# Late chunks of alpha, k and q landed token by token, with a ScalarE copy beside and transposes that write in order

## The chip, the cores and the metric

The kernel runs on one core of one Trainium2 chip. The metric is the device time of one execution, in microseconds. Numbers of the profile come from one profiled execution on the same chip.

## The reference

A gated linear attention recurrence, for batch 4, 8 heads, 768 tokens and head size 48, is followed by a two-layer block with a SiLU between:

```python
for t in range(S):
    state = alpha[:, :, t, :, None] * state + einsum('bhd,bhe->bhde', k[:, :, t], v[:, :, t])
    y[:, :, t] = einsum('bhd,bhde->bhe', q[:, :, t], state)
x = y.transpose(0, 2, 1, 3).reshape(B * S, H * D)     # 3072 x 384
h = x @ w_in                                          # w_in 384 x 2048
out = (h * (1 / (1 + exp(-h)))) @ w_out               # w_out 2048 x 384
```

q, k, v and alpha are fp32. The two weights arrive as 64-bit floats and are rounded on the chip.

## The kernel before

The tokens are cut into chunks of 128; with 4 batches there are NT = 24 chunks, numbered so that the four batches of one token range follow each other. The function `quotients` holds the whole fast path. Step n of its main loop runs the stages of chunk n (products, quotient, flip) and the later stages of chunk n-1 (land, scores, values, states). Between the stages, `fill` puts pieces of the two-layer block: `enter` (x times w_in, with sums that spare products), `leave` (times w_out). The first NA = 8 chunks are early ones; the 16 from chunk 8 on are late ones, and the change touches only these. The late stage begins with `settle`, which frees buffers of the first stage and makes three tiles, `quads`, one each for alpha, k and q (`at`, `kt`, `qt` in the profile).

**How a late chunk is loaded.** `load(n, name)` is called for each tensor as soon as the tensor of chunk n-1 has been transposed, since there is one tile for each. Line 486 issues four transfers of 96 KB for each tensor. A group of 32 partitions takes four heads of one parity (u); partition b of the group takes the four tokens 4b to 4b+3, so that each run is 4 x 48 elements, 768 bytes. The same data land twice: once in the partitions 64u to 64u+31 from column 32 on, and once in the next 32 partitions from column 0 on, so that the same columns of the two groups hold, for one token, the elements 0 to 31 and the elements from 32 on.

**How it is transposed.** `turned` (line 708) lets VectorE transpose blocks of 32 x 32: for head pair g and token j of the four, 32 partitions by 32 columns. What comes out is the head dimension over the partitions and the tokens along the row. As partition b held the tokens 4b to 4b+3, the results of one block go to every fourth element of the row.

**What comes of it.** `products` takes alpha (scan on line 734: products of decays from the end of the chunk), then k (kp on lines 749 and 751). `quotient` makes the other scan (line 764) and q's product (line 770). `flip` (line 780) transposes kp and writes it to DRAM (line 782, `flips`); in the next step `land` (line 790) reads it back as `kn`, in four transfers, for `states` (line 874), which adds the chunk to the recurrent state. `scores` multiplies kp and qp, ScalarE copies the results from PSUM (lines 818 and 821) and scales the state (line 836), GpSimd masks them (line 825), and `values` makes the chunk's output, which ScalarE copies into `xt` (line 863).

**What sets the order.** Each engine works through its own queue in order. A scheduler places the instructions of the traced program on the queues; from the late stage on, TensorE's matmuls are held in program order. All loads of chunks, the flips, the reads of kn and the loads of `audit` stand in one queue, SyncE's, and each waits there for what its buffer needs. `audit` reads alpha and the weights once more in pieces, from step 15 on, and checks their range with reductions on VectorE (line 697); its later pieces land in the three `quads` tiles. The outputs go through GpSimd's queue (line 1059).

PSUM banks: three for `enter` (ps_m), two for `leave` (ps_o), three for the attention (ps_a). ScalarE empties them with lines 950 (`enter`), 1054, 1073 and 1078 (`leave`) and 923 (the plain form of `enter`, with SiLU); VectorE with lines 958, 1056, 1088 and 1099. Line 1047 makes differences for `leave`.

Of the kernel before, what the change touches and what calls it, by code (L numbers as in the profile page):

```python
# [8 lines left out]
F32 = mybir.dt.float32  # L9
I32 = mybir.dt.int32  # L10
# [345 lines left out]
def quotients(  # L356
# [19 lines left out]
    nc = tc.nc  # L376
    dve, act, gps = nc.vector, nc.scalar, nc.gpsimd

    late = {}
# [14 lines left out]
    B, H, S, D = q.shape  # L394
    C = 128
    NCH = S // C
    NP = H // 2
    HD = H * D
# [3 lines left out]
    NT = B * NCH  # L402
# [9 lines left out]
    def pool(name, bufs=1, space=None):  # L412
        kw = {} if space is None else {"space": space}
        return ctx.enter_context(tc.tile_pool(name=name, bufs=bufs, **kw))
# [40 lines left out]
    NA = 2 * GB  # L455
# [8 lines left out]
    ctxs = {}  # L464

    def load(n, names="akq"):
        if n == NT:
            return
        c = ctxs.setdefault(n, dict(zip(("ci", "b"), divmod(n, B))))
        b, rows = c["b"], slice(c["ci"] * C, c["ci"] * C + C)  # L470
        for name, src in (("a", alpha), ("k", k), ("q", q)):
            if name not in names:
                continue
            x = src[b, :, rows, :]
            if n < NA:
                c[name] = nat[name][n % NIN]
                nc.sync.dma_start(c[name][:, :, 0:D], x.transpose([1, 0, 2]))
                continue

            c[name] = late["quads"][name]
            for u in range(2):
                for i in range(2):
                    r = 64 * u + 32 * i
                    nc.sync.dma_start(
                        c[name][r : r + 32, 32 * (1 - i) :][:, 0 : 4 * NP * D].rearrange(
                            "p (g c) -> p g c", g=NP),
                        x[u::2].rearrange("h (b j) d -> b h (j d)", j=4))

    NV = 2
    vns = [fix.tile([128, H, 64], F32, name=f"vn{i}") for i in range(NV)]
# [3 lines left out]
    def load_v(n):  # L496
        c = ctxs.setdefault(n, dict(zip(("ci", "b"), divmod(n, B))))
        x = v[c["b"], :, c["ci"] * C : c["ci"] * C + C, :].transpose([1, 0, 2])
        t = c["v"] = vns[n % NV]
        if n < NA:  # L500
            nc.sync.dma_start(t[:, :, 0:D], x)
            return
        nc.sync.dma_start(t[:, 0 : H // 2, 0:D], x[:, 0 : H // 2])
        for e in range(2):
            nc.sync.dma_start(t[CH * e : CH * e + CH, H // 2 :, 0:D], x[CH - CH * e : C - CH * e, H // 2 :])
# [7 lines left out]
    def fetch():  # L513

        if wide and sources:
# [4 lines left out]
            coming.append(bits)  # L520

    load(0)
    load(1)
    for i in range(4):
        fetch()
# [47 lines left out]
    quads = w_in.rearrange("p k (q i c) -> p i k q c", i=4, c=128)  # L573
# [83 lines left out]
    def audit():  # L657


        flat = alpha.rearrange("b h s d -> (b h s d)").rearrange("(p c) -> p c", p=128)  # L660
        assert 2 * HD <= 32 + 4 * NP * D
        todo = [(flat[:, c : c + AW], AW, 0) for c in range(0, flat.shape[1], AW)]
        if wide:
            todo += [(moe_w_in[t * 128 : t * 128 + 128, c : c + 512], 512, 1)
                     for c in range(0, DF, 512) for t in range(NKT)]
            todo += [(moe_w_out[f * 128 : f * 128 + 128, :], HD, 1) for f in range(NFT)]
        alone = sum(2 * x[1] > 32 + 4 * NP * D or x[2] == 0 for x in todo)
        for kind in (0, 1):
            n = sum(x[2] == kind for x in todo)
            if n:  # L670
                seen.append([fix.tile([128, n], F32, name=f"seen{kind}{i}") for i in range(2)])
        at = [0, 0]
        landed = []

        def begin(src, n, kind):
            at = len(landed)
            t = late["look"].tile([128, 512, 2], I32, name="bits").rearrange("p n w -> p (n w)") if (
                at < alone) else late["quads"]["akq"[at % 3]].bitcast(I32)
            if kind == 0:
                landed.append(t[:, 0:n].bitcast(F32))  # L680
                nc.sync.dma_start(landed[-1], src)
            else:
                nc.sync.dma_start(t[:, 0 : 2 * n], src.bitcast(I32))
                landed.append(t[:, 0 : 2 * n].rearrange("p (n w) -> p n w", w=2)[:, :, 1])

        for i, (src, n, kind) in enumerate(todo):

            while len(landed) < min(i + (1 if i + 1 < alone else 3), len(todo)):
                begin(*todo[len(landed)])
            x = landed[i]  # L690
            yield
            i = at[kind]
            at[kind] += 1
            for which, op in ((0, ALU.max), (1, ALU.min)):
                if kind == 1 or which == 0:
                    tc.keep_in_program_order(
                        dve.tensor_reduce(seen[kind][which][:, i : i + 1], x, axis=AX, op=op,  # L697
                                          apply_absolute_value=True))
# [5 lines left out]
        return t[:, 1 : NP * W + 1].rearrange("p (j c) -> p j c", c=W)[:, :, 0:C]  # L704

    def turned(x, to):
        x = x[:, 32:].rearrange("p (g j d) -> p g j d", j=4, d=D)
        dve.transpose(to.rearrange("p g (b j) -> p g j b", j=4), x[:, :, :, 0:32])

    def products(n):  # L710

# [28 lines left out]
        if n >= NA:  # L740
            ps["k"] = late["turn"].tile([128, NP, C], F32, name="turn")
            turned(c["k"], ps["k"])
            load(n + 1, "k")
# [414 lines left out]
    def go_on():  # L1158
# [3 lines left out]
        done += 1  # L1162

    audits = audit()
    done, bridged = 0, 0
    STEPS = NT + 1
# [4 lines left out]
    def settle():  # L1171

        first.close()
        late.update(look=pool("look"), part=pool("part"), turn=pool("turn"),
                    xc=pool("xc").tile([128, len(SUMS_X), TB], F32, name="xc"),
                    wx=pool("wx").tile([128, 8, NQ, 128], F32, name="wx"))
        quads = pool("quads")
        late["p"] = pool("p").tile([128, NP * W + 1], F32, name="p")
        late["quads"] = {name: quads.tile([128, 32 + 4 * NP * D], F32, name=f"{name}t") for name in "akq"}
        for name, t in late["quads"].items():  # L1180
            gps.memset(t, 1.0 if name == "a" else 0.0)
        load(NA)

    def fill(step, slot):

        at = step * SLOTS + slot
        if at < marks[0]:
            if at == SLOTS:
                next(conv[0])
            elif step >= 1:  # L1190
                convert(0, (at - SLOTS) * 3 // (marks[0] - SLOTS) + 1)
            return
        i = next(i for i, m in enumerate(marks[1:]) if at < m)
        a, b = [work_at[n] for n in ([0] + phases)[i : i + 2]]
        due = a + (b - a) * (at - marks[i] + 1) / (marks[i + 1] - marks[i])
        if at % 2 == 0 and step > 3 * GB + 2:
            next(audits, None)
        while work_at[done + 1] <= due and pieces[done][2] <= bridged:
            convert(0, 3 * (done // 2) + 6)
            convert(1, 3 * (done - 6) // 2)  # L1200
            go_on()

    for step in range(STEPS):
        if step == 1:
            load(NIN)
        stages = [[(scores, 1)], [(products, 0)], [(values, 1)], [(states, 1)]]
        if step == 1:

            stages = stages[1::-1] + stages[2:]
        elif step >= NA:  # L1210
            stages = [[(land, 1), (scores, 1)], [(products, 0)], [(quotient, 0)],
                      [(values, 1), (states, 1), (flip, 0)]]
        for slot, group in enumerate(stages):
            for stage, lag in group:
                n = step - lag
                if not 0 <= n < NT:
                    continue
                stage(n)
                if stage is values:
                    bridged = n + 1  # L1220
                if stage is states and n + 1 + NIN < NA:
                    load(n + 1 + NIN)
                if stage is states and n + NV < NT:
                    load_v(n + NV)
            if step * SLOTS + slot == (NA + 1) * SLOTS - 1:
                x = decayed.rearrange("p (o i c) -> p o i c", o=2, c=C)
                for r, o in later:
                    gps.memset(x[r, o, :, 0:CH], 0.0)
            fill(step, slot)
            if step * SLOTS + slot >= NA * SLOTS - 1 and conv_done[1] == NFT and not late:  # L1230
                settle()
# [82 lines left out]
```

## Time and profile before

| | us |
|---|---|
| median of 3 runs | 556.63 (556.30 to 557.37) |
| the profiled execution | 557.26 |
| its span, first to last instruction | 555.5 |
| TensorE matmul busy | 541.4 (97%) |
| VectorE busy | 445.4 (80%) |
| ScalarE busy | 208.5 (38%) |
| GpSimd busy | 76.1 (14%) |
| granted TensorE clock | 0.999 |

In the profile PE is TensorE's matmuls, PEld its weight loads, DVE is VectorE, ACT is ScalarE, POOL is GpSimd and SP is SyncE; a q behind an engine means its queue, where DMAs are issued. L708 is line 708 of the kernel. A group of instructions shows its busy time, the mean of one, and how long the engine stood idle just before it and what ended that. A line of waits gives the time in total, how often, and the longest. Idle time of an engine that isn't the bottleneck costs nothing.

### The profile page before, as it was taken

Reading aid. Unit: us, or ns where it says so; the run is one execution under the profiler, and the core shown is the slowest. Engines: PE = TensorE matmul, PEld = TensorE weight load, DVE = VectorE, ACT = ScalarE, POOL = GpSimd, SP = SyncE. Lnnn points to the kernel's source line nnn. Section 1 sums busy time; section 2 is a strip of 40 time slices with the busy share of each in tenths; the row PEclk is TensorE's granted clock in tenths of the full one; section 3 lists DMA queues with packets and bytes.
Section 4 is the critical chain, followed back from the end, with each engine's and each line's share of the span. In section 5 each row is a group of like instructions: output and inputs, shape, how many; then the busy total and the mean of one; then the engine's idle time right before and its main releaser. Section 6 shows DMA issues by size and latency. Waiting matters only on the chain. (4 is left out here: it accounts for less than half of the span.)

```text
span 555.5 us, 12640 instructions
## 1 busy us (share of the span) xinstructions
PE 541.4 (97%) x5026; PEld 489.7 (88%) x5026; DVE 445.4 (80%) x801; ACT 208.5 (38%) x466; POOL 76.1 (14%) x146
## 2 busy tenths in 40 slices
PE   6999999999999999999999999999999999999996
PEld 4788887998899999899999999988998999999996
DVE  5897788974999899997998986998884796945431
ACT  2556653223333253353353353344263342332100
POOL 3210000222210212021011021021121000001000
PEclk9999999999999999999999999999999999999999
DMA  9998971164454625355545654617642135500000
GB/s 215 246 249 210 232 195 33 47 161 116 117 136 125 159 63 138 86 145 149 139 112 139 193 139 120 191 27 183 170 137 91 54 91 169 172 11 22 10 24 30
DMA packets 99217, 70.09 MB, mean 126 GB/s; under 512 B 56272, under 2 KB 88656, under 8 KB 99152
## 3 DMA queue, kind: packets, MB, share of 16 engines
q1 hardware_dynamic: 97232, 65.30, 45.1%
q0 software_dynamic: 1920, 3.93, 2.0%
q8 instruction: 40, 0.66, 0.5%
q14 instruction: 25, 0.20, 0.1%
HBM read 61.34 MB, written 7.86 MB: 125 GB/s over the span
## 5 line engine op out<-in xcount | busy, mean ns | idle before, releaser
L388 PE MATMUL ps_o<-w_out,g 128*128 128x192 f32 x768 | 134.0, 328 | 0.5 <-DVE o L1056 0.5
L388 PEld LDWEIGHTS ps_o<-w_out,g 128*128 128x128 f32 x768 | 125.6, 190 | 3.5 <-DVE o L1056 1.0
L388 PE MATMUL ps_m<-xt,w_in 128*128 128x256 f32 x480 | 113.6, 383 | 1.5 <-ACT xt L863 1.1
L388 PEld LDWEIGHTS ps_m<-xt,w_in 128*128 128x128 f32 x480 | 89.1, 190 | 14.4 <-ACT xt L863 1.6
L388 PE MATMUL ps_o<-wt,g 128*128 128x192 f32 x576 | 99.7, 326 | 0.0
L388 PEld LDWEIGHTS ps_o<-wt,g 128*128 128x128 f32 x576 | 95.1, 190 | 1.6 <-issue 0.2
L388 PE MATMUL ps_m<-xc,w_in 128*128 128x256 f32 x288 | 70.7, 382 | 0.0
L388 PEld LDWEIGHTS ps_m<-xc,w_in 128*128 128x128 f32 x288 | 53.7, 190 | 7.0 <-DVE g L958 0.3
L1047 DVE TENSOR_TENSOR g<-g 128x512 f32<-128x512 f32 x72 | 50.1, 709 | 8.3 <-PE ps_o L388 8.3
L955 ACT ACTIVATE g<-g 128x1024 f32<-128x1024 f32 x32 | 33.1, 1056 | 61.2 <-DVE g L958 61.1
L1059 POOL DMA_DIRECT2D out_dram<-o x40 | 22.0, 551 | 219.5 <-DVE o L1056 113.7
L825 POOL TENSOR_SCALAR_AFFINE_SELECT g<-g 64x256 f32<-64x256 f32 x64 | 34.9, 546 | 124.4 <-ACT g L818 105.7
L388 PE MATMUL ps_m<-xc,wx 128*128 128x256 f32 x192 | 50.1, 383 | 1.0 <-DVE xc L586 1.0
L950 ACT COPY g<-ps_m 128x512 f32<-128x512 f32 x64 | 36.6, 588 | 37.0 <-PE ps_m L388 36.9
L388 PEld LDWEIGHTS ps_m<-xc,wx 128*128 128x128 f32 x192 | 35.2, 190 | 5.2 <-ACT u L1078 1.2
L958 DVE TENSOR_TENSOR g<-ps_m,g 128x512 f32<-128x512 f32 x56 | 37.1, 683 | 3.2 <-PE ps_m L388 2.7
L734 DVE TENSOR_TENSOR_SCAN u<-al,one 128x516 f32<-128x516 f32 x24 | 29.8, 1240 | 11.9 <-ACT al L731 11.6
L923 ACT ACTIVATE g<-ps_m 128x512 f32<-128x512 f32 x32 | 19.1, 597 | 41.7 <-PE ps_m L388 41.4
L950 ACT COPY part<-ps_m 128x512 f32<-128x512 f32 x32 | 18.9, 590 | 38.0 <-PE ps_m L388 24.0
L697 DVE TENSOR_REDUCE seen<-bits 128x1 f32<-128x512 int32 (+1 forms) x33 | 26.3, 823 | 5.7 <-DMA bits<-in_moe_w_in_dram 5.7
L764 DVE TENSOR_TENSOR_SCAN p<-al,inv 128x516 f32<-128x516 f32 x24 | 29.9, 1247 | 1.0 <-PE ps_a L388 0.3
L1056 DVE TENSOR_TENSOR o<-ps_o,u 128x192 f32<-128x192 f32 x24 | 8.5, 355 | 25.7 <-PE ps_o L388 22.8
(129 smaller groups left out, 648.5 us busy)
## 6 DMA issues: line engine op xcount, KB each, us to landing
bits<-in_moe_w_in_dram SPq DMA_DIRECT2D x24, 512.0 KB, 4.7
bits<-in_moe_w_out_dram SPq DMA_DIRECT2D x16, 384.0 KB, 3.9
at<-in_alpha_dram SPq DMA_DIRECT2D x64, 96.0 KB, 2.5
kt<-in_k_dram SPq DMA_DIRECT2D x64, 96.0 KB, 2.6
qt<-in_q_dram SPq DMA_DIRECT2D x64, 96.0 KB, 2.7
bits<-in_alpha_dram SPq DMA_DIRECT2D x9, 512.0 KB, 4.0
out_dram<-o POOLq DMA_DIRECT2D x40, 96.0 KB, 2.4
flips<-turn SPq DMA_DIRECT2D x12, 256.0 KB, 2.4
```

The lines of the kernel that those rows point to most:

```text
L388: in_order(nc.tensor.matmul(*args, **kw))
L697: dve.tensor_reduce(seen[kind][which][:, i : i + 1], x, axis=AX, op=op, apply_absolute_value=True))
L734: dve.tensor_tensor_scan(u[:, end - 1 :: -1], sg[:, end:0:-1], one[:, end:0:-1], 0.0, ALU.mult, ALU.add)
L764: dve.tensor_tensor_scan(p[:, 0:end], sg[:, 0:end], iv[:, 0:end], 0.0, ALU.mult, ALU.add)
L825: gps.affine_select(x, x, pattern=[[0, NP], [1, CH]], compare_op=ALU.is_ge, fill=0.0, base=0, channel_multiplier=-1)
L923: act.activation(gts[grp, h, pair][:, i : i + 2, q % 2, :], ps, AF.Silu)
L950: act.copy(to, ps)
L955: act.activation(x, x, AF.Silu)
L958: dve.tensor_tensor(to, a, b, op)
L1047: dve.tensor_tensor(cells(grp, h, pair, *to), cells(grp, h, pair, *x), cells(grp, h, pair, *y), ALU.subtract)
L1056: dve.tensor_tensor(o, x, y, ALU.add)
L1059: (gps if grp < NG - 1 else nc.sync).dma_start(out[r : r + C, c * HO : (c + 1) * HO], o)
```

## The change

The data of a late chunk land once. There is a transfer for each head, 8 for each tensor: partition b takes the tokens b, 32+b, 64+b and 96+b, each a run of 48 elements, 192 bytes. In a new stage, `beside`, ScalarE copies the elements 32 to 47 of each token from the partitions 64u to 64u+31 into the columns 0 to 15 of the next 32 partitions: two copies of 32 partitions by 256 elements for each tensor. The transposed block then holds 32 neighbouring tokens, and `turned` writes it to neighbouring elements. `beside` stands in the first slot of a step, ahead of `products`, for that step's own chunk. The tile loses its 32 extra columns, and `audit` takes the tile's new shape.

```diff
@@ load
             c[name] = late["quads"][name]
+            for g in range(NP):
+                for u in range(2):
+                    nc.sync.dma_start(c[name][64 * u : 64 * u + 32, g],
+                                      x[2 * g + u].rearrange("(j b) d -> b j d", b=32))
+
+    def beside(n):
+
+        for name in "akq" if NA <= n < NT else "":
             for u in range(2):
-                for i in range(2):
-                    r = 64 * u + 32 * i
-                    nc.sync.dma_start(
-                        c[name][r : r + 32, 32 * (1 - i) :][:, 0 : 4 * NP * D].rearrange(
-                            "p (g c) -> p g c", g=NP),
-                        x[u::2].rearrange("h (b j) d -> b h (j d)", j=4))
+                r = slice(64 * u, 64 * u + 32)
+                act.copy(ctxs[n][name][64 * u + 32 : 64 * u + 64, :, :, 0 : D - 32],
+                         ctxs[n][name][r, :, :, 32:D])
@@ audit
-        assert 2 * HD <= 32 + 4 * NP * D
+        assert 2 * HD <= 4 * NP * D
-        alone = sum(2 * x[1] > 32 + 4 * NP * D or x[2] == 0 for x in todo)
+        alone = sum(2 * x[1] > 4 * NP * D or x[2] == 0 for x in todo)
-                at < alone) else late["quads"]["akq"[at % 3]].bitcast(I32)
+                at < alone) else late["quads"]["akq"[at % 3]].rearrange(
+                    "p g j d -> p (g j d)").bitcast(I32)
@@ turned
-        x = x[:, 32:].rearrange("p (g j d) -> p g j d", j=4, d=D)
-        dve.transpose(to.rearrange("p g (b j) -> p g j b", j=4), x[:, :, :, 0:32])
+        dve.transpose(to.rearrange("p g (j b) -> p g j b", j=4), x[:, :, :, 0:32])
@@ settle
-        late["quads"] = {name: quads.tile([128, 32 + 4 * NP * D], F32, name=f"{name}t") for name in "akq"}
+        late["quads"] = {name: quads.tile([128, NP, 4, D], F32, name=f"{name}t") for name in "akq"}
@@ the main loop
-            stages = [[(land, 1), (scores, 1)], [(products, 0)], [(quotient, 0)],
+            stages = [[(land, 1), (beside, 0), (scores, 1)], [(products, 0)], [(quotient, 0)],
```

## The prediction

> **What bounds the kernel now.** I read the busy shares first, then the same by stretches of time, then what TensorE waited for, then the two queues that the change touches.
>
> ```profile
> PE 541.4 (97%) x5026; PEld 489.7 (88%) x5026; DVE 445.4 (80%) x801; ACT 208.5 (38%) x466; POOL 76.1 (14%) x146
> ```
>
> TensorE is busy 97% of 555.5 us. By stretches (columns: stretch, its length, then busy us of PE, PEld, DVE, ACT, POOL, then clock, DMA share, GB/s):
>
> ```profile
> 140.00:160.00 20.00, 19.52 (x244) 17.64 (x236) 19.44 (x33) 5.67 (x17) 3.40 (x5) 1.00 0.48 127
> 180.00:200.00 20.00, 20.00 (x211) 18.26 (x210) 17.71 (x36) 7.00 (x19) 5.85 (x10) 1.00 0.52 139
> ```
>
> While late chunks are under way (about 108 to 405 us) TensorE misses only some 2 us. VectorE is nearly full, but whether that matters is told by TensorE's own waits:
>
> ```profile
> PE ps_m L388 <- DVE xc L586: 1.0, 1, 1.0
> ...
> PE ps_a L388 <- DVE p L770: 0.5, 1, 0.5
> ...
> PE ps_m L388 <- DVE g L958: 0.4, 1, 0.4
> ```
>
> These three, 1.9 us together, are all that VectorE costs TensorE in that stretch. So a faster VectorE can win at most about 1.9 us, and anything that comes late for TensorE, whose late order is fixed, is lost in full. The operations concerned (line, engine, operation, out<-in and shapes, count | busy, mean ns | idle before):
>
> ```profile
> L708 DVE STREAM_TRANSPOSE al<-at 128x512 f32<-128x512 f32 x16 | 18.2, 1137 | 1.6 <-DMA at<-in_alpha_dram 1.5
> L708 DVE STREAM_TRANSPOSE turn<-kt 128x512 f32<-128x512 f32 x16 | 18.1, 1133 | 0.0
> L708 DVE STREAM_TRANSPOSE turn<-qt 128x512 f32<-128x512 f32 x16 | 17.8, 1110 | 0.3
> L780 DVE STREAM_TRANSPOSE turn<-kp 128x512 f32<-128x512 f32 x12 | 8.5, 708 | 0.1
> L818 ACT COPY g<-ps_a 128x256 f32<-128x256 f32 x32 | 10.4, 376 | 10.0 <-PE ps_a L388 10.0
> ```
>
> Last, SyncE's queue in time order (start, us from first to last issue, count), where all these loads are issued one behind another:
>
> ```profile
> 112.55 1.80 SPq L486 DMA_DIRECT2D kt<-in_k_dram  x4
> 114.45 1.81 SPq L486 DMA_DIRECT2D qt<-in_q_dram  x4
> 116.35 2.71 SPq L486 DMA_DIRECT2D at<-in_alpha_dram  x4
> ...
> 126.52 0.39 SPq L503 DMA_DIRECT2D vn<-in_v_dram  x1
> 127.01 1.26 SPq L505 DMA_DIRECT2D vn<-in_v_dram  x2
> 128.36 0.55 SPq L782 DMA_DIRECT2D flips<-turn  x1
> 129.00 1.40 SPq L486 DMA_DIRECT2D at<-in_alpha_dram  x2
> 131.44 1.74 SPq L790 DMA_DIRECT2D kn<-flips  x4
> ```
>
> and TensorE's matmuls of the states, which read kn:
>
> ```profile
> 140.03 0.52 PE L388 MATMUL ps_a<-vn,kn 128*32 128x48 f32 x32
> ...
> 156.79 0.52 PE L388 MATMUL ps_a<-vn,kn 128*32 128x48 f32 x32
> ...
> 173.00 0.52 PE L388 MATMUL ps_a<-vn,kn 128*32 128x48 f32 x32
> ...
> 189.20 0.52 PE L388 MATMUL ps_a<-vn,kn 128*32 128x48 f32 x32
> ...
> 210.61 0.52 PE L388 MATMUL ps_a<-vn,kn 128*32 128x48 f32 x32
> ```
>
> A load costs SyncE (114.45-112.55)/4 = 0.475 us, the next train again (116.35-114.45)/4 = 0.475. The first kn loads end their issue at 133.2 and are read at 140.03. The steps behind are 16.8, 16.2, 16.2 and then 21.4 us long; later ones are 20.5 to 22.6.
>
> [...] Line 708 writes every fourth fp32 and takes 1.13 us; line 780, which writes in order, 0.71[...] 96 KB loads land 2.5 to 2.7 us after issue, and SyncE's waits hold what is behind them. [...] the 0.475 us measured between issues is what counts here. [...] line 818 with 256 elements takes 376, and I take that.
>
> **The change part by part.** Late chunks are 16, with three tensors each.
>
> *Transposes in order.* 48 instructions drop from 1.13 to about 0.71 us (line 780's row): 48 x 0.42 = 20 us of VectorE. This lies beside TensorE's matmuls; only its 1.9 us of waits can shrink. One, of 0.5 us at 143.8, comes just after the loss worked out below and is swallowed by it. Of the other two I take 1.0 us. Bounds: 0 to 1.9.
>
> *ScalarE's copies.* 6 x 16 = 96 copies x 0.376 = 36 us on an engine busy 208 of 555 us, some 2.3 us more in a step of 16 to 22 us. Their own time is hidden in ScalarE's idle time. But each waits for a landing, and behind it in ScalarE's queue stand the evacuations of PSUM (lines 818, 821, 923, 950) and xt. The order of the changed program puts them mostly after such a copy-out and some microseconds after the expected landing. About 4 us of TensorE's work lies between filling a ps_m bank and needing it again in the later part (three banks, with 2.7 us of ps_o matmuls between), so waits of 1 to 2 us are covered; longer ones are the third rival. I take 0.
>
> *Half the bytes, twice the packets.* 24 transfers of 24 KB instead of 12 of 96 KB. The DMA share is about 0.5 in these stretches, and the bytes of a, k and q fall from 1180 to 590 KB a chunk. No price.
>
> *The issues.* Nothing hides these if SyncE is late. Each transfer has 128 runs before and after, so I keep 0.475 us apiece. The start: before, the first late load issues at 108.59 and flips at 128.36. In the changed order 48 small loads (chunks 8 and 9) and 6 of v stand ahead of flips: 48 x 0.475 = 22.8, two v trains of 1.85 (109.52 to 111.37) = 3.7, and two overlong issues, of 0.9 and 0.5 (2.71 for 1.80; 1.40 for 0.87), 27.9 in all, flips at 136.5. Before, SyncE waited in this stretch; after, it does not, and the transposes that the loads wait for stay ahead of it. The kn loads start about 2.5 us after flips (2.4 to 3.1), the last one 1.3 later, and land 2.8 after (the page's median): 136.5 + 2.5 + 1.3 + 2.8 = 143.1. TensorE wants kn at 140.0: **3.1 us lost**. Chunk 8's a is itself about 2.5 us later (4 more issues ahead, two copies), which holds line 1088 and so a ps_o bank by near 1 us; that is part of the 3.1, not added to it.
>
> Then each step issues 24 loads, 4 of kn, 3 of v and flips: 28 x 0.475 + 1.85 + 0.64 = 15.8, plus 0.4 of waiting for flips to land (2.5 less flips and three loads), plus overlong issues: six of them cost 5.9 us in 83 us, so 1.15 a step. That is 17.35 us against steps of 16.8, 16.2 and 16.2: **another 0.6 + 1.1 + 1.1 = 2.9 us**. The steps of 20.5 to 22.6 us that follow give SyncE slack again, also with two audit loads (18.3 us), so the loss stops.
>
> *Small things.* GpSimd's queue changes only in three memsets, 4% shorter, ahead of the first late load; TensorE's order stays as it was: 0.
>
> Sum: +3.1 + 2.9 - 1.0 = +5.0. The profiled execution took 557.26 us (span 555.5), so 562.3; it stood 0.6 above the median of 556.63, so 561.6 as a median.
>
> **Rivals.** *1, SyncE keeps up, no difference.* At the 0.43 us that one issue lasts and without overlong ones, flips go at 108.6 + 20.6 + 3.7 = 132.9 and the last kn lands at 139.5, just in time; a step needs 15 us. For it: only three short steps are tight. Against: the measured 0.475 holds train after train. Then 0 to -1: 555.6 to 556.6. *2, faster.* As in 1, and VectorE's 20 us take all its waits away: -1.9, so 554.7. The profile grants no more, since TensorE is busy 20.00 of 20 us nearly everywhere. *3, ScalarE blocks.* In every step q's copies wait longer than the spare few microseconds, since q is issued last; line 950's copies, then VectorE's line 958, then a ps_m bank come late. It decides where q lands over 3 to 4 us after ScalarE reaches it; 0.5 us in each of 16 steps on top of the issue loss gives +13, so 570. Against: it wants a slip in the long steps too, where SyncE has spare time. That the change doesn't do what it says (strided writes were not the cost) would leave the transposes at 1.13 and the time 1 us higher.
>
> **How the numbers follow.** SyncE late: 0.57, own range 558.5 to 566. ScalarE blocks as well: 0.18. No difference: 0.15. Faster: 0.10. A measurement of this kernel tells about 0.2%, 1.1 us, from no change; a little of rival 1 falls on each side of it. Chances: faster 0.11, same 0.13, slower 0.76. The range from 555.6 to 570 leaves out most of rival 2 and the tail of rival 3.
>
> **What would show it.** Right: line 708's mean near 0.71 us; TensorE waiting for DMA kn by flips near 140 us and in the next three steps, 6 us in all; SyncE without idle time from 108 to 190 us. Wrong: no wait on kn (rivals 1 and 2), issues shorter than 0.4 us, or waits ended by ScalarE or VectorE spread over 200 to 400 us (rival 3). The forecast falls if the issues of small runs cost other than 0.475 us: 0.05 us more is 2.4 us at the start and 1.6 in each of the short steps.

## The result, and the profile after

The changed kernel took 564.03 us as a median of 4 runs (563.23 to 566.08); the kernel before, run beside it, 557.0 (556.3 to 557.4). The ratio is 1.0134, with a 95% interval of 1.0112 to 1.0156: slower by 7.0 us. The profiled execution took 566.08 us (span 564.3), 8.8 more than that of before; it is the slowest of the four, so the steps below add up to more than the medians differ by.

The busy shares of the changed kernel, in the page:

```profile
PE 542.8 (96%) x5026; PEld 491.0 (87%) x5026; DVE 427.9 (76%) x801; ACT 249.8 (44%) x562; POOL 75.9 (13%) x146
```

VectorE lost 17.5 us of work and ScalarE gained 41.3. TensorE issues the same 5026 matmuls, and is 1.4 us busier. The groups by line (count | busy, mean ns | idle before them and what ended it):

```profile
L493 ACT COPY kt<-kt 32x256 f32<-32x256 f32 x32 | 12.9, 403 | 4.3 <-DMA kt<-in_k_dram 3.5
L493 ACT COPY at<-at 32x256 f32<-32x256 f32 x32 | 12.9, 402 | 21.8 <-DMA at<-in_alpha_dram 10.9 <-DVE st L885 3.9 <-DVE xc L587 3.1
L493 ACT COPY qt<-qt 32x256 f32<-32x256 f32 x32 | 12.9, 402 | 8.6 <-DMA qt<-in_q_dram 7.9
...
L713 DVE STREAM_TRANSPOSE al<-at 128x512 f32<-128x512 f32 x16 | 11.3, 707 | 8.8 <-ACT at L493 7.4 <-DMA kt<-in_k_dram 1.3
```

The transposition in order takes 0.71 us where the strided one took 1.13. What bounds the kernel is told by what TensorE waited for; its largest wait (total, times, longest) is new:

```profile
PE ps_a L388 <- DMA kn<-flips: 7.1, 4, 2.8
```

TensorE's timeline shows where (start, us, engine and line, instruction, count, then the wait just before it):

```profile
142.26 0.87 PE L388 MATMUL ps_a<-vn,kn 128*32 128x48 f32 x32 [2.79 <-DMA kn<-flips]
143.06 4.10 PE L388 MATMUL ps_o<-w_out,g 128*128 128x192 f32 x16
...
160.83 0.55 PE L388 MATMUL ps_a<-vn,kn 128*32 128x48 f32 x32 [0.60 <-DMA kn<-flips]
...
178.27 0.55 PE L388 MATMUL ps_a<-vn,kn 128*32 128x48 f32 x32 [1.02 <-DMA kn<-flips]
...
197.35 0.87 PE L388 MATMUL ps_a<-vn,kn 128*32 128x48 f32 x32 [2.67 <-DMA kn<-flips]
...
220.10 0.52 PE L388 MATMUL ps_a<-vn,kn 128*32 128x48 f32 x32
```

The first four reads of kn are late, and the fifth, after a longer step, is not. Beside the two long waits something else stands: 32 small matmuls take 0.87 us instead of 0.52, and sixteen of `leave` take 4.10 instead of the 2.87 of the kernel before. The windows of 20 us say why (columns as before; the clock is third from the end):

```profile
140.00:160.00 20.00, 17.74 (x192) 16.46 (x192) 14.69 (x29) 7.23 (x22) 2.69 (x5) 0.91 0.37 78
...
180.00:200.00 20.00, 17.33 (x188) 15.46 (x188) 12.38 (x25) 7.90 (x22) 4.33 (x6) 0.92 0.37 80
```

In both the granted clock is down to 0.91 and 0.92; in the clock records it is 0.5 for 3.41 us from 142.17 and again from 196.79. The cause of the late kn is in SyncE's queue (start, us from first to last issue, count):

```profile
107.36 1.76 SPq L485 DMA_DIRECT2D at<-in_alpha_dram  x4
...
113.20 4.81 SPq L485 DMA_DIRECT2D kt<-in_k_dram  x8
118.11 3.69 SPq L485 DMA_DIRECT2D qt<-in_q_dram  x8
...
136.47 0.55 SPq L787 DMA_DIRECT2D flips<-turn  x1
...
138.75 1.74 SPq L795 DMA_DIRECT2D kn<-flips  x4
...
154.05 1.53 SPq L787 DMA_DIRECT2D flips<-turn  x1
...
172.12 0.55 SPq L787 DMA_DIRECT2D flips<-turn  x1
...
178.94 4.91 SPq L485 DMA_DIRECT2D kt<-in_k_dram  x8
...
188.25 2.43 SPq L510 DMA_DIRECT2D vn<-in_v_dram  x2
190.77 0.56 SPq L787 DMA_DIRECT2D flips<-turn  x1
```

The first flip goes out at 136.47 instead of 128.36. From there SyncE, which has no gap longer than 0.6 us from 107 to about 208 us, needs 17.6, 18.1 and 18.7 us for a step that took TensorE 16.2 to 16.8 before.

**Where the 8.8 us are.** Both programs issue the same matmuls in the same order, so each can be set against its counterpart, and the delay read off where it jumps. The changed execution came to its first late kn 0.7 us ahead, mostly from the first 25 us, which differ from run to run. The four kn steps then add 2.97, 0.78, 1.21 and 2.85, together 7.8; the two stretches at half clock 1.6 and 1.3, together 2.9; three waits on VectorE that are gone give back 0.55, 0.93 and 1.20, together 2.7; a new wait on g by L960 near 369 us and small things add 0.5. That makes 7.8 at the last matmul. From there to the end of the span it takes 5.7 us instead of 4.7: another 1.0.

The terms are places where the delay grew, and not all are separate costs. SyncE hardly stood still up to 208 us, so the next kn came when SyncE brought it: what TensorE lost to the first stretch at half clock made the next wait shorter by as much. Only the second stretch, 1.3 us, adds to the end. That is read from the order in the trace; no run tried it. Also, each delay at a kn is 0.18 us more than the wait that is listed there (2.97 for 2.79, 0.78 for 0.60, and so on). This fits how matmuls in a row overlap: sixteen of 0.33 us each take 2.87, while idle time is counted only from the end of the one before.

### The profile page after: what moved, and what is told of

It is laid out like the page before. It is cut to its first block, busy times and chain, and to the rows that moved or that the text cites. A ratio compares the mean times of both kernels' runs of the same rounds, so it can differ in the third digit from the quotient of the medians.

```text
span 564.3 us, 13229 instructions
## 1 busy us (share of the span) xinstructions
PE 542.8 (96%) x5026; PEld 491.0 (87%) x5026; DVE 427.9 (76%) x801; ACT 249.8 (44%) x562; POOL 75.9 (13%) x146
## 5 line engine op out<-in xcount | busy, mean ns | idle before, releaser
L388 PE MATMUL ps_o<-w_out,g 128*128 128x192 f32 x768 | 136.7, 332 | 1.1 <-DVE o L1061 0.5
L388 PEld LDWEIGHTS ps_o<-w_out,g 128*128 128x128 f32 x768 | 127.8, 193 | 4.6 <-DVE o L1061 0.8
L1052 DVE TENSOR_TENSOR g<-g 128x512 f32<-128x512 f32 x72 | 48.2, 682 | 11.8 <-PE ps_o L388 11.8
L960 ACT ACTIVATE g<-g 128x1024 f32<-128x1024 f32 x32 | 33.0, 1055 | 52.7 <-DVE g L963 52.6
L955 ACT COPY g<-ps_m 128x512 f32<-128x512 f32 x64 | 37.0, 587 | 33.2 <-PE ps_m L388 32.8
L955 ACT COPY part<-ps_m 128x512 f32<-128x512 f32 x32 | 18.8, 589 | 25.0 <-PE ps_m L388 18.6
```

The source lines that it names most:

```text
L388: in_order(nc.tensor.matmul(*args, **kw))
L955: act.copy(to, ps)
L960: act.activation(x, x, AF.Silu)
L1052: dve.tensor_tensor(cells(grp, h, pair, *to), cells(grp, h, pair, *x), cells(grp, h, pair, *y), ALU.subtract)
```

## The experiments

The theory to test: SyncE's issues are the cost, 0.475 us each; small packets, the copies and the writes are not. Rivals: the small packets make landings late (packets), or ScalarE, held by its copies, makes its other work late (ScalarE). In what follows "the last matmul" is the delay of the last matmul against the profiled kernel before (as the late loads began, these executions already stood between 1.5 us ahead of it and 0.3 behind, which is in the figure), and "the ending" is the time from it to the end of the span (4.7 us before).

**Flips and kn through GpSimd.** The changed kernel, with two lines edited:

```diff
-        nc.sync.dma_start(c["flip"], t.rearrange("p c j d -> p (c j d)"))
+        gps.dma_start(c["flip"], t.rearrange("p c j d -> p (c j d)"))
-                nc.sync.dma_start(c["kn"][32 * i : 32 * i + 32], x[i])
+                gps.dma_start(c["kn"][32 * i : 32 * i + 32], x[i])
```

> The changed kernel, but the write of flips and the four reads of kn are issued from GpSimd's queue, so that they no longer stand behind the small loads in SyncE's. If the loss is that kn is issued late behind the small loads: the four waits on kn (7.1 us) and the slower clock after the two long ones (3.4 us in the profiled run) go; SyncE then needs 13.6 us a step and keeps up; 554.5 to 557.5 us. If the small runs land late or ScalarE's copies hold the work up: TensorE still waits, for kp, p or the copies from PSUM, and the time stays above 560.

Measured: 559.1 us, 1.0041 (1.0027 to 1.0056). No wait on kn is left; the last matmul is 0.6 us later than before, and the ending is 5.7. The packets, the copies and the bytes are those of the changed kernel, so what made it slow is that flips and kn stood behind loads in one queue. The time lies between the two forecasts; 1.0 us of it is the ending. One small loss remains, in ScalarE's timeline:

```profile
299.51 0.40 ACT L493 COPY kt<-kt 32x256 f32<-32x256 f32 x1 [5.82 <-DMA kt<-in_k_dram]
299.94 0.48 ACT L868 COPY xt<-ps_a 128x384 f32<-128x384 f32 x1
```

A copy waits 5.8 us for k to land, and the copy to xt behind it comes late; TensorE waits 1.2 us for xt. That is the prediction's third rival, once in 16 steps.

**Twice as many transfers, nothing else.** The kernel before, each of its 12 transfers a chunk split into two of two heads; runs of 768 bytes, double landing and strided writes stay:

```diff
-                    nc.sync.dma_start(
-                        c[name][r : r + 32, 32 * (1 - i) :][:, 0 : 4 * NP * D].rearrange(
-                            "p (g c) -> p g c", g=NP),
-                        x[u::2].rearrange("h (b j) d -> b h (j d)", j=4))
+                    for g in range(0, NP, 2):
+                        nc.sync.dma_start(
+                            c[name][r : r + 32, 32 * (1 - i) :][:, 0 : 4 * NP * D].rearrange(
+                                "p (g c) -> p g c", g=NP)[:, g : g + 2],
+                            x[u::2].rearrange("h (b j) d -> b h (j d)", j=4)[:, g : g + 2])
```

> The kernel before, each of its transfers of a late chunk split in two (two heads each): 8 issues for each tensor as in the changed kernel, but runs of 768 bytes, the double landing, strided transposes and no copies. If the number of issues alone is the cost, at 0.475 us each: kn late by some 3 us at 140 us and again in the next three steps, and none of VectorE's gain: 564 to 567 us. If an issue with 64 runs is cheaper (0.31 us, as the first of a train), less than half of that: 557 to 560. If small runs or ScalarE's copies are the cost: 557, as before.

Measured: 566.28 us, 1.0161 (1.0148 to 1.0174). TensorE's waits:

```profile
PE ps_a L388 <- DMA kn<-flips: 4.7, 4, 1.8
```

The same four waits come back with no copy of ScalarE and no 192-byte run: the first flip goes at 136.69, as late as in the changed kernel. The last matmul is 6.7 us late and the ending 7.2 us long. The time falls into the forecast range partly by luck: the kn steps add 5.4 us, and the longer ending 2.4. Three waits on VectorE are gone here too, and give back the same 0.55, 0.93 and 1.20 us as in the changed kernel, though the writes are as slow as before (VectorE is busy 446.4 us, 445.4 before): TensorE comes late to these places, and finds the data there. (Waits of 0.4 on g and 0.6 on xc stand at other places.) So in the changed kernel these 2.7 us can't be put down to the faster writes. A transfer of 64 runs costs SyncE no less than one of 128: eight of k take 4.80 us here and 4.81 in the changed kernel.

**Writes in order, nothing else.** The kernel before with the transposition's writes in order; the tokens of a late chunk then stand in another order than they should, and the arithmetic is otherwise the same:

```diff
-        dve.transpose(to.rearrange("p g (b j) -> p g j b", j=4), x[:, :, :, 0:32])
+        dve.transpose(to.rearrange("p g (j b) -> p g j b", j=4), x[:, :, :, 0:32])
```

> The kernel before, with the transposes of late chunks writing in order, nothing else: the tokens of a late chunk then stand in another order in their row, so what is computed for them differs, but no instruction, load or wait is added. The gain of VectorE alone: line 708 at 0.71 us instead of 1.13, 20 us less of VectorE; TensorE's three waits on VectorE in the late stage shrink: 0 to 1.9 us faster, 555 to 557. If VectorE's pace mattered beyond the waits that the profile shows: below 554.

Measured: 554.16 us, 0.9947 (0.9934 to 0.9959), or 2.9 us faster. The waits on p, g and xc that VectorE ended in the late stage are gone, and the last matmul is 3.1 us earlier, 0.4 of which was there before the late stage began. So what the change was worth on VectorE alone is 2.7 us, above the bound of 1.9, and all of it stands at these three places: 0.55, 0.93 and 1.21 us, where the kernel before lists waits of 0.48, 0.39 and 0.96.

**The copies, nothing else.** The kernel before, with ScalarE's six copies a chunk in the new stage, writing the values that already stand there:

```diff
+            for u in range(2):
+                act.copy(x[64 * u + 32 : 64 * u + 64, :, :, 0 : D - 32],
+                         x[64 * u : 64 * u + 32, :, :, 32:D])
...
-            stages = [[(land, 1), (scores, 1)], [(products, 0)], [(quotient, 0)],
+            stages = [[(land, 1), (beside, 0), (scores, 1)], [(products, 0)], [(quotient, 0)],
```

> The kernel before, with ScalarE's 96 copies added in the changed kernel's stage: they write what has landed there already. If the loss is the issues: the copies cost ScalarE 39 us beside TensorE and nothing in time, 556.5 to 558. If ScalarE's queue, held at the copies until the loads land, is part of the loss: 559 or more, with TensorE's waits ended by ScalarE.

Measured: 557.96 us, 1.002 (1.0013 to 1.0027). 96 copies of 0.40 us, 38.6 us of ScalarE, move the last matmul by 0.2 us. The ending is 6.0 us instead of 4.7, which is the rest.

**Half of the loads through GpSimd.** The changed kernel; flips and kn stay on SyncE:

```diff
-                    nc.sync.dma_start(c[name][64 * u : 64 * u + 32, g],
+                    (gps if u else nc.sync).dma_start(c[name][64 * u : 64 * u + 32, g],
```

> The changed kernel with the transfers of every second head of alpha, k and q (12 of 24 a chunk) issued by GpSimd instead of SyncE; the flip transfer and the kn loads stay on SyncE. Theory A (SyncE's issues are the cost): SyncE's step falls from 17.4 by 12 x 0.475 = 5.7 us to under 12, flips and kn come some 5 us or more ahead of need, no wait for kn is left; the time is that of the kernel before plus the later ending (1.0) plus 0.2 to 0.6, 558 to 558.8. Theory B (GpSimd's queue is the next one): its 76 us of arithmetic now stand behind issues, g or u come late, waits of TensorE on POOL-fed tiles of 1 us or more in several steps, 560 to 566. Theory C (small packets, not issues): kn still late, 563 to 565.

Measured: 566.94 us, 1.0201 (1.018 to 1.0222), a miss for the price, though not for the wait: flips go out at 124.0, and no wait on a kn of the late stage is left. The groups show what took its place:

```profile
L485 POOL DMA_DIRECT2D at<-in_alpha_dram x64 | 35.0, 553 | 63.0 <-DVE al L713 36.7 <-ACT g L826 13.1 <-ACT g L823 7.1
...
L493 ACT COPY qt<-qt 32x256 f32<-32x256 f32 x32 | 12.9, 403 | 36.8 <-DMA qt<-in_q_dram 32.5 <-DVE turn L713 4.0
L493 ACT COPY kt<-kt 32x256 f32<-32x256 f32 x32 | 12.9, 402 | 35.4 <-DMA kt<-in_k_dram 35.0
```

An issue keeps GpSimd for 0.553 us, and stands there behind GpSimd's arithmetic. The halves of k and q land later, and ScalarE's idle time ahead of their copies grows from 4.3 and 8.6 us to 35.4 and 36.8. What stands behind them comes late: TensorE waits 3.6 us for `part` (L955), 4.6 for xt (L868; 1.1 before), 1.4 for u. At 220.65 us the clock also drops for 3.41 us, which costs 1.6: sixteen matmuls of `leave` take 4.52 us from 220.67. This is the third rival in full, made by late landings and not by the copies' own time: what TensorE waits for is fed by ScalarE and VectorE, and not by GpSimd as expected.

**Copies by need.** The flips-through-GpSimd kernel, with each tensor's two copies moved from the one stage to just ahead of its own transposition:

```diff
-            stages = [[(land, 1), (beside, 0), (scores, 1)], [(products, 0)], [(quotient, 0)],
+            stages = [[(land, 1), (scores, 1)], [(products, 0)], [(quotient, 0)],
+                    beside(n, "a")
                     turned(c[name], tokens(sg))
+            beside(n, "k")
             turned(c["k"], ps["k"])
+            beside(n, "q")
             turned(c["q"], q)
```

> The run with flips and kn on GpSimd (559.1, 1.0041 of before) with ScalarE's six copies a chunk taken from one stage at the start of the step and put each right ahead of the transposition that reads it. Theory A (what is left of the loss there is ScalarE held by a late landing, 5.8 us at 294 us, and the 1.2 us wait on xt behind it): that wait is gone, the end of the matmuls is about 0.5 to 1.2 us earlier, 557.8 to 558.6. Theory B (the remainder is the program's ending alone): no change, 559 to 559.4. Theory C (the copies now wait behind other work of ScalarE and hold VectorE's transpositions, whose results are wanted soon after): new waits on al, k or q based tiles, 560 or more.

Measured: 560.63 us, 1.0063 (1.0042 to 1.0084): the hold is not removed. Near 294 us ScalarE again stands 6.4 us for k, TensorE 1.8 for xt, and the clock then drops for 3.41 us, which costs another 1.6. A wait of 1.3 us on g by L958 near 198 us is new: the third theory, in one place. Where the copies stand in the traced program made no difference to this hold: k's eight loads are issued only at 294.5.

**q alone through GpSimd.** The changed kernel with `(gps if name == "q" else nc.sync)` in the same place.

> The changed kernel with only q's 8 transfers a chunk issued by GpSimd. Theory A (issues, 0.475 us each): SyncE's step falls from 17.4-18.7 by 3.8 to 13.6-14.9 us, under the shortest step of 16.2; two chunks of q are ahead of the first flips, 16 x 0.475 = 7.6 us, so flips go at about 129 instead of 136.5, no wait on kn; 558 to 559. Theory B (GpSimd's queue blocks): waits on POOL-fed tiles, above 560. Theory C (packets): 563 to 565.

Measured: 561.52 us (560.09 to 566.85), 1.0106 (1.0073 to 1.014). Flips go at 127.8 (129 expected) and no late kn is waited for, but ScalarE stands 47.6 us ahead of q's copies, and TensorE waits 2.5 us for g by L955 and 1.3 for xt. (A wait of 1.7 us on g by GpSimd's L818 is in the first 25 us, ahead of all late chunks.) The last matmul is 1.8 us late and the ending 6.7. The issue theory is right on kn and the second on the price, though the tiles waited for are ScalarE's.

**Half of the loads through ScalarE.** As with GpSimd, with `(act if u else nc.sync)`.

> The changed kernel with the transfers of every second head of alpha, k and q issued by ScalarE instead of SyncE. Theory A (only SyncE's queue was short of time): the kn wait is gone. Theory B (an issue takes time of whichever queue it stands in): 12 x 0.475 = 5.7 us a step more on ScalarE's queue, which also waits there for the buffers of the transposition before; the copies out of PSUM behind it come late by 3 to 6 us in a step, TensorE waits for ACT-fed tiles (xt, g) in most of the 16 late steps, 0.5 to 2 us each, 566 to 590. I take B, 575.

Measured: 558.68 us, 1.0036 (1.0024 to 1.0049). I took 575 and was wrong. In SyncE's queue:

```profile
123.27 0.35 SPq L787 DMA_DIRECT2D flips<-turn  x1
```

No late kn is waited for, and the ending is 5.7. The last matmul is 0.6 us earlier than before, but this execution was 1.5 us ahead as the late loads began, so the late stage lost 0.9. An issue takes ScalarE's queue about as long as SyncE's (1.90 us for four of k; SyncE's four of alpha take 1.80 in the same execution), yet the landings are in time: ScalarE stands 9.6 us ahead of k's copies and 4.3 ahead of q's. It has the idle time for 5.7 us more a step; the new waits are on o (0.8) and xt (0.7, and 0.3 more at an old one), and 0.2 on u.

**How many tensors.** Three kernels with the change made for alpha alone, for q alone, and for both (shown); the other tensors are loaded and transposed as before:

```diff
             c[name] = late["quads"][name]
+            if name in "aq":
+                y = c[name][:, 32:].rearrange("p (g j d) -> p g j d", j=4, d=D)
+                for g in range(NP):
+                    for u in range(2):
+                        nc.sync.dma_start(y[64 * u : 64 * u + 32, g],
+                                          x[2 * g + u].rearrange("(j b) d -> b j d", b=32))
+                continue
```

> The kernel before with the change made for alpha alone: 8 transfers by head and two ScalarE copies a chunk, its 16 transpositions write in order; k and q as before. Theory A (SyncE's issues are the cost, 0.475 us each): 32 loads stand ahead of the first flips instead of 24 (48 in the full change), which gives 108.6 + 32 x 0.475 + 3.7 + 1.4 = 128.9 us, where VectorE brings flips at 128.4 anyway; a step of SyncE is 13.5 us against the shortest of 16.2. No wait on kn, no loss from issues; VectorE is 6.7 us less busy and part of its three waits (1.9 us) goes: 555.5 to 556.8 of 556.9, or 1.0 more if the program ends later. Theory B (small packets themselves delay landings, or ScalarE held by the copies): a third of the loss of the full change, 2 to 3 us, 559.

Measured: 559.02 us, 1.0035 (1.0021 to 1.0048). No wait on kn. The last matmul is 0.9 us late and the ending 5.7. That is above the issue theory's number and is the rival's 559, but the rival's mechanism would show more with two tensors, which the third kernel denies. The loss is in waits of 0.3 to 0.5 us on g, xt and u near 119, 235 and 360 us; why alpha alone has them is open.

> The same for q alone. Theory A: as for alpha alone, 555.5 to 556.8 (1.0 more if the ending is later); no wait on kn. Theory B: 559. If ScalarE's copies are what hurts, q is the worst of the three, since its transfers are issued last and are awaited longest: TensorE's waits on g by L955 or xt by L868 would show it.

Measured: 557.06 us, 1.0 (0.999 to 1.001). No wait on kn, the last matmul 0.8 us earlier, the ending 5.7. Flips went at 133.3 and not at 128.9, since q's second train of loads waited for its tile; kn, wanted at 140.3, was still in time.

> The same for alpha and q, k as before. Theory A: 40 loads ahead of the first flips, flips at 108.6 + 40 x 0.475 + 3.7 + 1.4 = 132.7 us and the last kn landed at 139.3, against 140.0 where TensorE wants it; a step of SyncE is 15.4 us against 16.2. So still no wait on kn, or one under 0.5 us, and VectorE is 13.4 us less busy: 554.5 to 556.5 (1.0 more if the ending is later). The loss is a threshold, not a slope: 0, 0, 7 us of kn waits for one, two and three tensors. Theory B: two thirds of the full loss, 561 to 562.

Measured: 556.53 us, 0.999 (0.9981 to 0.9998), the fastest of these kernels that leaves nothing of the computation out, and 0.1% ahead of the kernel before, barely clear of the noise. SyncE's queue:

```profile
132.41 0.55 SPq L800 DMA_DIRECT2D flips<-turn  x1
...
134.81 1.74 SPq L808 DMA_DIRECT2D kn<-flips  x4
```

and TensorE's first read of kn, without a wait:

```profile
139.75 0.52 PE L388 MATMUL ps_a<-vn,kn 128*32 128x48 f32 x32
```

Flips at 132.4 against 132.7 worked out. With one, two and three tensors the waits on kn are 0, 0 and 7.1 us: a threshold, as the issue theory has it. The second read comes 0.3 us late, too short a gap for the list of waits, so this kernel stands close to the threshold. Two thirds of the transpositions are faster; the last matmul is 1.5 us earlier, 0.8 of which was there as the late loads began, and the ending takes 1.0 back.

## Why the prediction was right, and where its sizes were off

The forecast of 561.6 us, slower, was right in its mechanism and 2.4 us short. Some of its sizes came out by luck. Point by point:

- **Flips at 136.5, first loss 3.1.** Flips went at 136.47, but two errors cancel there: the loads began at 107.36 instead of 108.59, and took 29.1 us to the flips instead of 27.9. The delay was 3.0, and again two things moved together: kn was read 0.8 us sooner than the 143.1 worked out, and TensorE stood there 0.7 us sooner than 140.0.
- **SyncE's step of 17.35 us, losses 0.6 + 1.1 + 1.1.** This is the term that was too small. The steps took 17.6, 18.1 and 18.7, and from the first late kn to the fourth TensorE lost 5.9 us against the kernel before, where 2.9 were forecast. The pitch of 0.475 us held; the overlong issues did not. They cost 1.2, 2.1 and 2.3 us in the three steps, where 1.15 a step was allowed: in the last, eight loads of k took 4.91 us instead of 3.70 and two of v 2.43 instead of 1.27. With twice as many transfers and nothing else, the steps took 17.5, 17.2 and 17.4, close to the forecast.
- **The loss stops in longer steps.** It did: no wait at 220.1 or later.
- **VectorE's gain, 1.0 and at most 1.9.** This bound failed: the writes alone won 2.7. The three waits read from the list were the right ones, but the idle time listed is less than the delay that it stands for (1.8 us of it against 2.7). In the changed kernel the three waits are gone as well, but lateness alone does that, as the split transfers show.
- **What strided writes cost.** The prediction set 1.13 us with every fourth element written beside 0.71 in order, from two lines of the kernel before. The kernel that changes nothing but the order shows the difference at one line: 0.704 to 0.707 us instead of 1.110 to 1.137.
- **ScalarE's copies at nothing.** Their own time costs 0.2 us. They took 0.402 us each; the trace row used, copies of 256 elements out of PSUM on 128 partitions, gave 0.376. The third rival didn't come about in the changed kernel, but did wherever GpSimd issued loads, and once with flips and kn through GpSimd.
- **Half the bytes, twice the packets, no price.** Right: with flips and kn in another queue, the same packets cost nothing that shows: no wait on kn is left, and the last matmul is 0.6 us late, with a wait of 1.2 on xt.
- **Not in the sum at all:** the half clock after the two long waits, of which 1.3 us reached the end in the profiled execution, a wait on g near 369 us, and the longer ending, 1.0. The wait on u by L1093 near 118 us (line 1088 before) was foreseen as near 1 us and took 0.3.

Summed in the terms of the prediction, for the profiled executions: 8.9 us were lost from just ahead of the first late kn to the fourth (6.0 forecast). The first stretch at half clock and the first of the waits on VectorE are inside this figure. Behind it come 1.3 of clock, 0.5 of g and small things and 1.0 of ending, none of them forecast, and -2.1 of waits on VectorE (-1.0 forecast). The start is -0.7.

## What to carry to other kernels

Count the DMA issues of each queue in each step, and price them from the pitch inside the queue's own trains, 0.475 us here: when what a step issues exceeds the step (17.6 to 18.7 us against 16.2 to 16.8), what stands last in that queue comes late, and twice as many transfers made it worse at half the bytes (flips at 136.47 us instead of 128.36). Before paying for an engine's time in issues, find a queue with idle time whose own work isn't waited for at that place, or change only so many tensors as the queue can bear; here the best of such moves won back most of the loss, and none came out more than 0.1% ahead of the kernel before. A delay adds to the end only where the next thing waited for isn't late anyway. Some of TensorE's waits, of 1.5 to 2.8 us, were followed by 3.41 us at half clock, which cost 1.3 to 1.6 us each time.

## What the runs showed of the hardware that was not expected

**Half clock followed some waits and not others.** In the changed kernel the two stretches at half clock lasted 3.41 us each, from 142.17 and 196.79. They came just behind waits of 2.79 and 2.67 us, and in the 3.41 us ahead of each TensorE's matmuls left 2.70 and 2.10 us idle. With half of the loads through GpSimd such a stretch came behind a wait of 1.52 us, but none behind one of 3.0 us (two of them in 565 us would have brought the mean clock to 0.994; it was 0.997). Copies by need had one behind a wait of 1.83 us, and q alone through GpSimd one in its first stage, where a wait of 1.7 stands (mean clock 0.995). The split transfers waited up to 1.8 us on kn, and their clock was 1.00 in every stretch up to 540 us. So the length of a wait alone did not tell whether half clock followed; what does is open.

**The ending differs between programs.** From the last matmul to the end of the span it took 4.7 us before, 4.6 to 4.7 in two of the other kernels, 5.7 to 5.8 in the changed kernel and five others, and 5.9, 6.0, 6.7 and 7.2 in the rest, with the same work in it. The sequencers' last semaphore instructions start later: SyncE's first one 3.50 us after the last matmul in the changed kernel, and 1.39 before. The packet records hint at why. Of the packets that the profile counts to the instruction queue q14, two start after the last matmul in the kernel before and four in the changed one; where the ending is 4.6 to 4.7 there are two or three, elsewhere three to five. No run tried this cause; the ending costs the changed kernel 1.0 us.

**The overlong issues went with instruction packets.** The page of the changed kernel lists 40 packets of 16 KB on another instruction queue:

```profile
q8 instruction: 40, 0.66, 0.5%
```

Between 105 and 405 us, 22 of SyncE's issues last over 0.8 us, and 21 of these have such a packet under way; of 441 issues of at most 0.6 us, 10 have. In all thirteen kernels it is 221 of 228. In the changed kernel 21 of the 23 packets in this stretch met an overlong issue, in the kernel before 16 of 25. The queue that issued with hardly a pause met nearly all of them. That is the term which the prediction had too small, as it took their number from the kernel before. That the packets cause the hold is not shown; they come together.

**The size of a transfer did not show in its issue.** On SyncE eight issues of 24 KB and 128 runs took 3.69 us, or 4.81 with an overlong one among them, and eight of 48 KB and 64 runs 3.70 and 4.80; on GpSimd one took 0.553 us of the engine.
